# Moving the fourth batch's keys and values to a later place, and splitting the second batch's v copies between two engines, in an attention and mixture-of-experts kernel

## The chip, the cores and the metric

The kernel runs on one core of one Trainium2 chip. The metric is the device time of one execution in microseconds (us), given as the median of several runs; the range of the runs stands in brackets. Every run has a state: fast, slow, or unknown where a kernel was run only once. No run here is slow. Four kernels (e5, e6, e11, e12) have a single run of unknown state; from these only the trace is read, and their times are not compared. A ratio of two kernels is the mean time of one kernel's fast runs over that of the other's of the same rounds, so it is not quite the ratio of the medians that are quoted.

Engines carry the profile's names: PE (TensorE, matmuls), PEld (its weight loads), DVE (VectorE), ACT (ScalarE), POOL (GpSimd), SP (SyncE). All times "at" some microsecond are read from the start of the profiled span of that kernel.

## The reference, cut to what matters

```python
# q, k, v: [8 batches, 8 heads, 576 rows, 64]
def phi(x):                      # relu, times cosine and sine of the row's angle: 64 -> 128 features
    r = np.maximum(x, 0.0); return np.concatenate([r * cos, r * sin], axis=-1)
q_p, k_p = phi(q), phi(k)
kv  = einsum('bhsf,bhsd->bhfd', k_p, v);  z = k_p.sum(axis=2)
num = einsum('bhsf,bhfd->bhsd', q_p, kv)
den = einsum('bhsf,bhf->bhs', q_p, z) + 1e-6
x = (num / den) as [4608 tokens, 512]
P = exp(x @ w_gate), then 8 rounds of row and column normalisation
out = sum over 8 experts e of  P[:, e] * (relu(x @ w1[e]) @ w2[e])   # 512 -> 1024 -> 512
```

## The kernel before

The kernel has three stages: the attention of eight batches, the balancing of P, and the experts. So that TensorE never idles in the first stage, the first expert's two matrix products for batch `j` run as "block" `j`, cut into 16 slots (0 to 7 make `h`, 8 to 15 make `y`), and the attention of batch `j + 1` is put between these slots. A list says what goes where:

```python
        def at(block, slot, fn, *args):
            todo.setdefault((block, slot), []).append((fn, args))
# ... cut: after the FFN part of each slot, the tasks of that slot run in the order of registration
```

Tasks are `prep_q`, `prep_k` (relu), `prep_kp` and `prep_v` (k features, copy of v; `prep_kv` is both), `sums` (the kv and z products), `denominators`, `attend`. Moving a task in the list thus moves its work on three engines at once, and what was written later stands behind it: in e3 below, a ScalarE eviction stands behind a relu that waits 1.46 us for its load, which costs TensorE 0.39 us; in e9, VectorE's work stands 2.16 us behind a q product that waits for its buffer.

From the third batch on, q features are transposed by a DMA (a transfer by the DMA engines) on SyncE's queue, not by TensorE:

```python
            if by_dma:                                   # b >= 2
                qTs[b, hk] = q_pTs[(b * HK + hk) % len(q_pTs)]
                turned = nc.sync.dma_start(
                    out=qTs[b, hk], in_=q_p[:].rearrange("p c a d -> p (c a d)"),
                    transpose=True,
                )
```

Some of the targets are lent parts of larger tiles: in the trace the transpose of the fourth batch's third q (`hk` 2) is `acc_lo<-q_p`, and that of its fourth and last q is `acc_hi<-q_p`. The `denominators` task needs all four of them.

The next batch's inputs are loaded by GpSimd's DMA queue, six loads of 288 KB, each held back until the VectorE instruction that was written last before it has run:

```python
        def load(b, half, names="qkv", held_back=False):
            for name in names:
                # ... cut: a new tile x
                i = nc.gpsimd.dma_start(out=..., in_=...)
                if held_back:
                    after(ve.last, i)
```

And the part of the schedule for block 1 that the argument touches (batch 3 counts as the "fourth batch", batch 4 as the "fifth"):

```python
                for slot, fn, hk in (
                    (4, prep_q, 0), (5, prep_q, 1), (8, prep_k, 0), (8, prep_q, 2),
                    (9, prep_k, 1), (10, prep_kv, 0), (10, prep_k, 2), (12, prep_q, 3),
                    (12, prep_kv, 1), (12, prep_k, 3), (13, prep_kv, 2), (14, prep_kp, 3),
                    (14, prep_v, 3),
                ) if j == 1 else ( ... )
                # ... cut
                at(j, 15 if j == 1 else 14, sums, b + 1, 0)
            if j == 1:
                for name in "qkv":
                    for half in range(2):
                        at(j, 12, load, b + 2, half, name, True)   # the fifth batch's six loads
```

The last VectorE instruction of slot 12 before the loads is the v copy of `prep_kv 1` (`prep_k` runs on ScalarE). The loads hang on whatever that list has last.

Of the kernel before, what the change touches and what calls it, by code (L numbers as in the profile page):

```python
# [25 lines left out]
def kernel(  # L26
# [91 lines left out]
    te, ve, se = bound  # L118
# [62 lines left out]
    with ExitStack() as p1:  # L181
# [265 lines left out]
        def sums_begun(b, half):  # L447

            W_ = D + 1 if b else D
            if half == 0 and b:  # L450
                kvs[b] = (
                    kv_pool.tile([P, HK, 2, D], F16, name="kv_sb"),
                    kv_pool.tile([P, H, 32], F16, name="zsel"),
                )
            kv_ps = [ps_s.tile([P, 512], FP32, name="small_ps") for hh in range(2)]
            for i in range(2):
                k_p, v_aug = kps.pop((b, 2 * half + i))
                for c in range(C):
                    for hh in range(2):
                        te.matmul(  # L460
                            out=kv_ps[hh][:, i * W_ : (i + 1) * W_],
                            lhsT=k_p[hh * HP : (hh + 1) * HP, c].rearrange("p a d -> p (a d)"),
                            rhs=v_aug[hh * HP : (hh + 1) * HP, c, 0:W_],
                            start=(c == 0),
                            stop=(c == C - 1),
                        )
            return kv_ps

        def sums_made(b, half, kv_ps):
            kv_sb, zsel = kvs[b]  # L470
            W_ = D + 1 if b else D
            for hh in range(2):
                kv_v = kv_ps[hh][:, 0 : 2 * W_].rearrange("p (hk d) -> p hk d", d=W_)
                se.copy(out=kv_sb[:, 2 * half : 2 * half + 2, hh, :], in_=kv_v[:, :, 0:D])
                if b:
                    ve.tensor_tensor(
                        out=zsel[:, 4 * half + hh : 4 * half + 4 : 2, :],
                        in0=zmask[:, 4 * half + hh : 4 * half + 4 : 2, :],
                        in1=kv_v[:, :, D : D + 1].to_broadcast([P, 2, 32]),
                        op=ALU.mult,  # L480
                    )
# [106 lines left out]
        def at(block, slot, fn, *args):  # L588
            todo.setdefault((block, slot), []).append((fn, args))
# [62 lines left out]
        for j in range(B):  # L652
            b = j + 1
            if j == 0:

                def sums_first(half):
                    sums_made(1, half, sums_begun(1, half))

                for hk in range(HK):
                    for i in range(3):  # L660
                        at(0, (5, 6, 6, 7)[hk], turn, 1, hk, i, i != 1)
                    if hk == 0:
                        at(0, 5, prep_q, 1, 3)
                    if hk == 2:
                        at(0, 6, prep_v, 1, 0, se.copy)
                        at(0, 6, prep_v, 1, 2, ve.tensor_copy)
                    if hk == 3:
                        at(0, 7, prep_v, 1, 1, se.copy)
                        at(0, 7, prep_v, 1, 3, ve.tensor_copy)
                for half in range(2):  # L670
                    at(0, 7, sums_first, half)
                at(0, 8, denominators, 1)
                at(0, 10, gates, 0)
                for hk in range(HK):
                    at(0, 11 + hk, attend, 1, hk)
            elif b < B:
                if j == 1:
                    at(0, 13, load, b + 1, 0, "q", True)
                    for hk in range(HK):
                        if hk >= 2:  # L680
                            at(j, 0, prep_k, b, hk, False)
                        at(j, 0, prep_kp, b, hk)
                        at(
                            j, (0, 0, 1, 3)[hk], prep_v, b, hk,
                            (ve.tensor_copy, se.copy)[hk // 2],
                        )
                    for name, half in (("q", 1), ("k", 0), ("k", 1), ("v", 0), ("v", 1)):
                        at(j, 0, load, b + 1, half, name, True)
                    at(j, 3, sums, b, 0)
                    at(j, 5, sums, b, 1)  # L690
                else:
                    at(j, 0, sums, b, 1)
                at(j, 6 if j == 1 else 3, denominators, b)
                for hk in range(HK):
                    at(j, (9, 10, 12, 13)[hk] if j == 1 else 6 + 2 * hk, attend, b, hk)
            if j:
                at(j, 5, gates, j)
            if j == 0:
                for half in range(2):
                    at(j, 3, load, b + 1, half)  # L700
                for slot, fn, hk, *args in (
                    (8, prep_q, 0), (11, prep_k, 0), (12, prep_q, 1), (12, prep_k, 1),
                    (13, prep_q, 2), (14, prep_q, 3),
                ):
                    at(j, slot, fn, b + 1, hk, *args)
            elif b + 1 < B:
                for slot, fn, hk in (
                    (4, prep_q, 0), (5, prep_q, 1), (8, prep_k, 0), (8, prep_q, 2),
                    (9, prep_k, 1), (10, prep_kv, 0), (10, prep_k, 2), (12, prep_q, 3),
                    (12, prep_kv, 1), (12, prep_k, 3), (13, prep_kv, 2), (14, prep_kp, 3),  # L710
                    (14, prep_v, 3),
                ) if j == 1 else (
                    (4, prep_q, 0), (5, prep_k, 0), (5, prep_q, 1), (6, prep_k, 1),
                    (7, prep_q, 2), (8, prep_kv, 0), (8, prep_k, 2), (9, prep_q, 3),
                    (10, prep_k, 3), (10, prep_kv, 1), (12, prep_kv, 2), (13, prep_kv, 3),
                ) if j == 2 else (
                    (3, prep_k, 0), (4, prep_q, 0), (4, prep_k, 1), (5, prep_q, 1),
                    (7, prep_kv, 0), (7, prep_k, 2), (7, prep_q, 2), (9, prep_q, 3),
                    (9, prep_k, 3), (9, prep_kv, 1), (11, prep_kv, 2), (13, prep_kv, 3),
                ):  # L720
                    at(j, slot, fn, b + 1, hk, *((se.copy,) if fn is prep_v else ()))
                at(j, 15 if j == 1 else 14, sums, b + 1, 0)
            if j == 1:
                for name in "qkv":
                    for half in range(2):
                        at(j, 12, load, b + 2, half, name, True)
            elif j and b + 2 < B:
                for half in range(2):
                    at(j, 11 + half, load, b + 2, half, "qkv", True)
        y_pss = {}  # L730
        for j in range(B - 1):
            if j:
# [435 lines left out]
    for e in range(1, E):  # L1168
        if e == 2:
            se = nc.scalar  # L1170
        w = w_next
        for n in range(NU):
# [28 lines left out]
            if e == 1 and n == 0:  # L1201
# [9 lines left out]
                ve = nc.vector  # L1211
# [42 lines left out]
```

## Time and profile before

| what | value | where it is read |
|---|---|---|
| time | 982.96 us (982.31 to 983.07, 3 runs) | the runs |
| profiled span | 980.3 us | the page |
| PE busy | 967.1 us, 99% | the page, busy time |
| PE's share of the chain that ended last | 94% | the page, chain of waits |
| PE waits in the first 110 us that the change can touch | about 3.4 us | timeline of PE |
| first matmul of the balancing stage | 165.64 us | timeline of PE |

These lines are from the page of the kernel before: busy time of the engines, the granted TensorE clock in tenths in 40 slices of the span, and the shares of the chain of waits.

```profile
PE 967.1 (99%) x7871; PEld 674.9 (69%) x7871; DVE 806.6 (82%) x1834; ACT 564.3 (58%) x1262; POOL 60.6 (6%) x82
PEclk9999999999999999999999999999999999999999
PE 94%; DVE 2%; ACT 2%; DMA 1%; POOL 0%; issue 0%; ACTq 0%; SPq 0%; POOLq 0%
```

TensorE is the bound (967.1 of 980.3 us busy), and its granted clock is 9 tenths or more in all 40 slices (mean 0.999). The change alters none of its 7871 matmuls, only their order.

The timeline of PE shows the waits. Columns are start in us, duration in us, engine, line (L109 is the helper through which all these instructions pass), operation, tile written <- tiles read, sizes, count, and in brackets the idle time just before and what ended it. First the second batch's sums in block 0 (kernel before):

```profile
31.69 0.44 PE L109 MATMUL small_ps<-acc_lo,k_p 64*128 64x65 f16 x17 [0.34 <-DVE acc_hi L109]
32.87 1.03 PE L109 MATMUL small_ps<-acc_lo,k_p 64*128 64x65 f16 x54 [0.74 <-ACT acc_lo L109]
33.84 1.04 PE L109 MATMUL y_ps<-w2e,hT 128*128 128x512 f16 x4
```

Here PE waits 0.34 us for VectorE and 0.74 us for ScalarE's copy of v. The next lines are the same view of the kernel before, in blocks 1 and 2:

```profile
58.68 0.46 PE L109 MATMUL small_ps<-hl,acc_hi 96*128 96x192 f16 x3 [0.23 <-ACT rb L109]
...
67.50 0.46 PE L109 MATMUL small_ps<-acc_lo,k_p 64*128 64x65 f16 x18 [0.18 <-DVE acc_lo L109]
68.16 0.46 PE L109 MATMUL small_ps<-acc_lo,k_p 64*128 64x65 f16 x18 [0.21 <-DVE k_p L109]
...
72.39 0.35 PE L109 MATMUL small_ps<-acc_hi,zsel 128*32 128x192 f16 x6 [0.46 <-DMA acc_hi<-q_p]
72.66 1.90 PE L109 MATMUL h_ps<-xT,w1e 128*128 128x512 f16 x8
```

The third batch's attend waits for ScalarE (`rb`). The fourth batch's first sums wait twice for VectorE. The fourth batch's denominators wait 0.46 us for the DMA that fills `acc_hi`.

The last thing to look at is that DMA. These lines are the DMA issues of the kernel before between 64.4 and 69 us: out <- in, queue, operation, count, median us from issue to landing.

```profile
acc_lo<-q_p SPq DMA_TRANSPOSE x1, 3.3
acc_hi<-q_p SPq DMA_TRANSPOSE x1, 6.3
```

And this is the timeline of POOL, where the fifth batch's loads are issued, the first of them at 65.99 us, released by the v copy (`acc_lo`) on VectorE:

```profile
65.99 1.43 POOL L202 DMA_DIRECT2D q_ld<-in_q_dram  x2 [11.32 <-DVE acc_lo L109]
```

Both transposes move 288 KB. The one that was issued before the loads landed after 3.3 us; `acc_hi` was issued at 66.08 us, just behind the first load, and took 6.3 us.

### The profile page before, as it was taken

To read this page: it belongs to the slowest core of one execution; us is meant where nothing else is said; L and a number is where in the kernel's file an instruction comes from. 1 tells how busy PE (TensorE), PEld (TensorE's weight loads), DVE (VectorE), ACT (ScalarE), POOL (GpSimd) and SP (SyncE) were. 2 spreads that over 40 slices of the span, in tenths; PEclk is the share of its full clock that TensorE was granted. 3 is DMA by queue.
4 is the path that set the end of the run, shared out by engine and by line. 5 is a ranking of instruction groups with operands and counts; after the bars stand their busy time and mean duration, and the time that the engine had idled before them with its cause. 6 is when DMAs were issued, how large, how long until landed. Compare 5 with 4: busy or idle time off the path is not lost.

```text
span 980.3 us, 20270 instructions
## 1 busy us (share of the span) xinstructions
PE 967.1 (99%) x7871; PEld 674.9 (69%) x7871; DVE 806.6 (82%) x1834; ACT 564.3 (58%) x1262; POOL 60.6 (6%) x82
## 2 busy tenths in 40 slices
PE   9999999989999999999999999999999999999997
PEld 6545444457777777777777777777777777777775
DVE  7767774788989888988888888988888888988887
ACT  5767665467776555555555555555555555555551
POOL 6231110010000000000000000000000000000001
PEclk9999999999999999999999999999999999999999
DMA  9999881730113400223103401223103401104435
GB/s 165 184 158 172 150 134 28 145 65 33 42 33 68 93 25 25 60 59 66 49 25 69 92 25 28 63 58 66 46 25 76 85 25 34 40 26 120 127 87 129
DMA packets 80336, 73.54 MB, mean 75 GB/s; under 512 B 33264, under 2 KB 72176, under 8 KB 80240
## 3 DMA queue, kind: packets, MB, share of 16 engines
q0 software_dynamic: 27232, 30.94, 20.2%
q1 hardware_dynamic: 52768, 41.06, 16.9%
q8 instruction: 61, 1.00, 0.4%
q14 instruction: 35, 0.29, 0.1%
q10 hardware_dynamic: 240, 0.26, 0.1%
HBM read 83.12 MB, written 12.98 MB: 98 GB/s over the span
## 4 chain that ended last, share of the span: by engine, by line
PE 94%; DVE 2%; ACT 2%; DMA 1%; POOL 0%; issue 0%; ACTq 0%; SPq 0%; POOLq 0%
PE rows_ps L109 34%; PE h_ps L109 28%; PE copied_ps L109 11%; PE p_ps L109 11%; PE y_ps L109 6%; PE small_ps L109 4%; DMA acc_hi<-q_p 1%; ACT hT L109 0%; ACT acc_lo L109 0%; DVE acc_hi L927 0%; POOL hs_last L942 0%; DVE P_tok L109 0%; DMA out_dram<-acc_lo 0%; DVE colp L109 0%; ACT u L109 0%
## 5 line engine op out<-in xcount | busy, mean ns | idle before, releaser
L927 DVE SCALAR_TENSOR_TENSOR acc_lo<-rows_ps,P_tok,acc_lo 128x512 f32<-128x512 f32 (+1 forms) x322 | 203.0, 639 | 74.4 <-PE rows_ps L109 74.3
L109 PEld LDWEIGHTS <-H 128*128 128x128 f16 x2080 | 203.0, 98 | 83.1 <-issue 1.2
L863 ACT CAST u<-h_ps 128x384 f16<-128x384 f32 x288 | 137.6, 478 | 131.2 <-PE h_ps L109 131.2
L109 PEld LDWEIGHTS <-w1e 128*128 128x128 f16 x1632 | 156.4, 98 | 66.4 <-issue 6.3
L857 DVE CUSTOM_DVE_ANT_0 H<-p_ps,u 128x384 f16<-128x384 f32 x329 | 180.8, 549 | 7.0 <-PE p_ps L109 6.6
L109 PEld LDWEIGHTS <-hs 128*128 128x128 f16 x1500 | 146.5, 98 | 56.2
L109 PE MATMUL h_ps<-S,w1e 128*128 128x384 f16 x672 | 164.1, 326 | 1.1 <-ACT u L109 0.9
L109 PE MATMUL p_ps<-xT,T 128*128 128x384 f16 x672 | 164.1, 326 | 0.1
L109 PE MATMUL rows_ps<-V,H 128*128 128x256 f16 x1000 | 150.0, 273 | 0.7 <-DVE acc_hi L927 0.7
L109 PE MATMUL h_ps<-xT,w1e 128*128 128x384 f16 (+1 forms) x616 | 150.0, 350 | 0.1
L109 PE MATMUL rows_ps<-w2e,hs 128*128 128x256 f16 x1000 | 150.0, 273 | 0.0
L895 ACT ACTIVATE H<-h_ps 128x384 f16<-128x384 f32 x144 | 70.6, 490 | 95.1 <-PE h_ps L109 95.1
L109 PEld LDWEIGHTS <-T 128*128 128x128 f16 x1008 | 98.1, 98 | 29.3 <-issue 2.8
L109 PE MATMUL rows_ps<-w2e,H 128*128 128x256 f16 (+1 forms) x568 | 91.2, 285 | 0.0
L876 ACT COPY copied_ps<-h_ps 128x384 f32<-128x384 f32 x144 | 67.5, 469 | 35.3 <-PE h_ps L109 35.3
L886 ACT ACTIVATE H<-copied_ps 128x384 f16<-128x384 f32 x144 | 70.8, 492 | 20.4 <-PE copied_ps L109 20.4
L109 PE MATMUL h_ps<-S,T 128*128 128x384 f16 x336 | 81.8, 325 | 0.3 <-ACT copied_ps L109 0.3
L109 PE MATMUL copied_ps<-xT,w1e 128*128 128x384 f16 x336 | 82.1, 326 | 0.0
L109 PE MATMUL copied_ps<-w2e,H 128*128 128x256 f16 x504 | 75.5, 272 | 0.0
L109 PE MATMUL rows_ps<-V,hs 128*128 128x256 f16 x500 | 75.0, 272 | 0.0
L927 DVE SCALAR_TENSOR_TENSOR acc_lo<-copied_ps,P_tok,acc_lo 128x256 f32<-128x256 f32 x126 | 60.0, 476 | 0.5
L927 DVE SCALAR_TENSOR_TENSOR acc_hi<-rows_ps,P_tok,acc_hi 128x512 f32<-128x512 f32 (+1 forms) x56 | 41.2, 736 | 20.5 <-PE rows_ps L109 19.7
(147 smaller groups left out, 950.0 us busy)
## 6 DMA issues: line engine op xcount, KB each, us to landing
S<-x_saved SPq DMA_DIRECT2D x108, 192.0 KB, 2.4
out_dram<-acc_lo SPq DMA_DIRECT2D x62, 128.0 KB, 2.4
w1e<-in_moe_w_dram POOLq DMA_DIRECT2D x7, 1024.0 KB, 8.9
w2e<-in_moe_w_dram POOLq DMA_DIRECT2D x7, 1024.0 KB, 9.7
q_ld<-in_q_dram POOLq DMA_DIRECT2D x16, 288.0 KB, 6.4
k_ld<-in_k_dram POOLq DMA_DIRECT2D x16, 288.0 KB, 8.2
v_ld<-in_v_dram POOLq DMA_DIRECT2D x16, 288.0 KB, 9.4
x_saved<-S SPq DMA_DIRECT2D x18, 192.0 KB, 1.9
```

Source lines behind the costliest of these rows:

```text
L109: i = getattr(self.engine, name)(*args, **kwargs)
L857: latest = ve._custom_dve(TENSOR_ADD_SAT, out=out, in0=ps[:, 0:TU], in1=t[:], s0=FP32_MAX, s1=0.0)
L863: se.copy(out=t[:], in_=ps[:, 0:TU])
L876: se.copy(out=Y[:, 0:TU], in_=X[:, 0:TU])
L886: se.activation(out=h11, in_=Y[:, 0:TU], func=AF.Relu)
L895: se.activation(out=h12, in_=X[:, 0:TU], func=AF.Relu)
L927: ve.scalar_tensor_tensor(out=a, in0=rows, scalar=P_tok[:, g, self.e : self.e + 1], in1=a, op0=ALU.mult, op1=ALU.add,)
```

## The change

The intent is to remove those waits. Part A, in block 0, gives the first two v copies of the second batch to ScalarE and VectorE in turn, so that the first sums can start before the last transposes of q. Part B puts the fourth batch's k and v work later in block 1 (from slot 10 instead of 8), its sums into block 2, and its attends from slot 8 of block 2 instead of 6; the fifth batch's work in block 2 moves back by one slot.

```diff
 # part A (block 0)
                 for hk in range(HK):
+                    if hk == 3:
+                        at(0, 7, sums_first, 0)
                     for i in range(3):
                         at(0, (5, 6, 6, 7)[hk], turn, 1, hk, i, i != 1)
                     ...
-                    if hk == 2:
-                        at(0, 6, prep_v, 1, 0, se.copy)
-                        at(0, 6, prep_v, 1, 2, ve.tensor_copy)
-                    if hk == 3:
-                        at(0, 7, prep_v, 1, 1, se.copy)
-                        at(0, 7, prep_v, 1, 3, ve.tensor_copy)
-                for half in range(2):
-                    at(0, 7, sums_first, half)
+                    if hk >= 2:
+                        at(0, 4 + hk, prep_v, 1, 2 * hk - 4, se.copy)
+                        at(0, 4 + hk, prep_v, 1, 2 * hk - 3, ve.tensor_copy)
+                at(0, 7, sums_first, 1)
 # part B (blocks 1 and 2)
+                elif j == 2:
+                    at(j, 0, prep_kv, b, 3)
+                    at(j, 1, sums, b, 0)
+                    at(j, 3, sums, b, 1)
 ...
-                at(j, 6 if j == 1 else 3, denominators, b)
+                at(j, 6 if j == 1 else 5 if j == 2 else 3, denominators, b)
 ...              # attends of block 2: from slot 8 instead of 6
                 # block 1
-                    (4, prep_q, 0), (5, prep_q, 1), (8, prep_k, 0), (8, prep_q, 2),
-                    (9, prep_k, 1), (10, prep_kv, 0), (10, prep_k, 2), (12, prep_q, 3),
-                    (12, prep_kv, 1), (12, prep_k, 3), (13, prep_kv, 2), (14, prep_kp, 3),
-                    (14, prep_v, 3),
+                    (4, prep_q, 0), (5, prep_q, 1), (8, prep_q, 2), (10, prep_k, 0),
+                    (11, prep_k, 1), (11, prep_kv, 0), (12, prep_q, 3), (12, prep_k, 2),
+                    (13, prep_kv, 1), (13, prep_k, 3), (15, prep_kv, 2),
 ...              # block 2: the fifth batch's list, one slot later
-                at(j, 15 if j == 1 else 14, sums, b + 1, 0)
+                if j > 1:
+                    at(j, 15 if j == 2 else 14, sums, b + 1, 0)
 ...              # block 2's own loads one slot later too
```

The six loads of the fifth batch are still registered for slot 12 of block 1. But in the new list the last VectorE instruction of slot 12 is the q feature product of `prep_q 3`, because `prep_kv 1` has moved to slot 13.

More of the change, by code (lines that the diff above doesn't have):

```diff
@@ L690 @@
                     at(j, 5, sums, b, 1)
+                elif j == 2:
+                    at(j, 0, prep_kv, b, 3)
+                    at(j, 1, sums, b, 0)
+                    at(j, 3, sums, b, 1)
                 else:
                     at(j, 0, sums, b, 1)
-                at(j, 6 if j == 1 else 3, denominators, b)
+                at(j, 6 if j == 1 else 5 if j == 2 else 3, denominators, b)
                 for hk in range(HK):
-                    at(j, (9, 10, 12, 13)[hk] if j == 1 else 6 + 2 * hk, attend, b, hk)
+                    at(j, (9, 10, 12, 13)[hk] if j == 1 else (8 if j == 2 else 6) + 2 * hk, attend, b, hk)
             if j:
@@ L707 @@
                 for slot, fn, hk in (
-                    (4, prep_q, 0), (5, prep_q, 1), (8, prep_k, 0), (8, prep_q, 2),
-                    (9, prep_k, 1), (10, prep_kv, 0), (10, prep_k, 2), (12, prep_q, 3),
-                    (12, prep_kv, 1), (12, prep_k, 3), (13, prep_kv, 2), (14, prep_kp, 3),
-                    (14, prep_v, 3),
+                    (4, prep_q, 0), (5, prep_q, 1), (8, prep_q, 2), (10, prep_k, 0),
+                    (11, prep_k, 1), (11, prep_kv, 0), (12, prep_q, 3), (12, prep_k, 2),
+                    (13, prep_kv, 1), (13, prep_k, 3), (15, prep_kv, 2),
                 ) if j == 1 else (
-                    (4, prep_q, 0), (5, prep_k, 0), (5, prep_q, 1), (6, prep_k, 1),
-                    (7, prep_q, 2), (8, prep_kv, 0), (8, prep_k, 2), (9, prep_q, 3),
-                    (10, prep_k, 3), (10, prep_kv, 1), (12, prep_kv, 2), (13, prep_kv, 3),
+                    (5, prep_q, 0), (6, prep_k, 0), (6, prep_q, 1), (7, prep_k, 1),
+                    (8, prep_q, 2), (9, prep_kv, 0), (9, prep_k, 2), (10, prep_q, 3),
+                    (11, prep_k, 3), (11, prep_kv, 1), (13, prep_kv, 2), (14, prep_kv, 3),
                 ) if j == 2 else (
@@ L720 @@
                 ):
-                    at(j, slot, fn, b + 1, hk, *((se.copy,) if fn is prep_v else ()))
-                at(j, 15 if j == 1 else 14, sums, b + 1, 0)
+                    at(j, slot, fn, b + 1, hk)
+                if j > 1:
+                    at(j, 15 if j == 2 else 14, sums, b + 1, 0)
             if j == 1:
@@ L728 @@
                 for half in range(2):
-                    at(j, 11 + half, load, b + 2, half, "qkv", True)
+                    at(j, 11 + (j == 2) + half, load, b + 2, half, "qkv", True)
         y_pss = {}
```

## The prediction

> **What bounds it.** TensorE. The page gives PE 967.1 of 980.3 us busy and 94% of the chain of waits; the granted clock is 1.0. In the timeline of PE, four 512-column matmuls take 0.87 us, 217 ns each[...]. The change only reorders PE's instructions. So it can only remove or add PE waits in the first 110 us; everything later shifts rigidly.
>
> **Where those waits are** (timeline of PE; loss = start-to-start distance less that of the same sequence where nothing waits):
> - A, 30.55 to 33.84: second batch's sums wait 0.34 for VectorE and 0.74 for the ScalarE copy of v. Loses about 1.4.
> - B1, 57.4 to 59.7: third batch's second attend waits for ScalarE (rb), which stood until 57.09 for the landing of the fourth batch's k. Loses 0.75.
> - B2, 66.3 to 68.5: fourth batch's first sums wait for VectorE's k_p and v copies. Loses 0.64.
> - B3, 72.39: denominators wait for the transpose of the fourth batch's last q, landed 72.34. Loses 0.64.
>
> **Change B (fourth batch later), about -1.2 us.**
> - B1 goes: ScalarE's first k relu now follows the rb copies.
> - B2 goes: the sums move from slot 15 to slot 1 of the next block, where by my addition VectorE (k_p 0.67, v copy 0.37 apart) has just finished.
> - B3 stays in part. PE reaches the last heads at 72.1 by the old clock. The fifth batch's loads hang on VectorE's last instruction in slot 12; that is now q_p (64.6), not the v copy (65.7), so they are issued 1.2 us earlier. The last transpose is still issued near 66.1, behind two loads rather than one. Before, it took 6.26 us instead of about 3.3. [...]I expect landing at 72.3 to 73.5, a wait of 0.2 to 1.4.
> - VectorE then has about 11 us of work before the fifth batch's second sums; it just fits, with a possible new wait up to 0.3.
>
> Sum of B: -2.0 + 0.8.
>
> **Change A (v copies split, first sums before the last turns), about +0.6 us.** The first sums start at 31.05 (first v copy ends 31.00). The last turn needs a PSUM buffer that the first sums hold: about 0.3 wait. Worse, ScalarE now does two kv_sb copies (0.43) and two q_pT evictions (0.74) before its second v copy (0.66), which ends near 33.7 (before: 32.82). The second sums end near 34.4, against 33.84.
>
> **Prediction: 982.3 us**, 80% range 981.2 to 983.6 (before 982.96). Faster by over 2%: 0.01; within 2%: 0.98; slower by over 2%: 0.01.
>
> **What the profile would show.** Right: a PE wait of about 1.1 us near 32.6 for ScalarE's v copy, the first y_ps matmul near 34.4; no PE wait at the attends near 57 to 60 or at the sums near 66 to 69; a PE wait of 0.2 to 1.4 in the fourth batch's denominators for the transpose into acc_hi. Wrong for A: first y_ps before 33.9. Wrong for B: denominators without wait, or waiting over 2 us.
>
> **What would make it wrong.** The transpose landing after three or more loads (3 us wait, slower overall); VectorE falling behind in block 2; ScalarE's late hT evictions stalling h_ps buffers; waits in the later balancing stage moving by themselves.

Two clauses that did not come from traces of this case are cut out of it, as marked. No term of the sum goes with them: -2.0 + 0.8 us for B and +0.6 us for A, on 982.96 us, come to 982.36, put on record as 982.3. The landing at 72.3 to 73.5 us and the wait of 0.2 to 1.4 us in B3 stand as my estimate, from the 6.26 and 3.3 us named there.

## The result, and the profile after

| | before | after |
|---|---|---|
| time, median (range, runs) | 983.02 us (982.31 to 985.69, 4) | 992.57 us (991.80 to 993.43, 4) |
| profiled span | 980.3 us | 990.7 us |
| mean granted clock | 0.999 | 0.994 |
| first matmul of the balancing stage | 165.64 us | 175.93 us |
| from there to the end | 814.7 us | 814.8 us |

The ratio is 1.0092, 95% interval 1.0072 to 1.0113. That is within 2%, but the kernel became 9.6 us slower where it was predicted to become 0.7 us faster, and 992.57 lies far outside the range. The last two rows say that everything happened before the balancing stage: PE arrives there 10.29 us later, and the rest takes as long as before.

The page of the kernel after, the same three lines:

```profile
PE 969.6 (98%) x7871; PEld 675.4 (68%) x7871; DVE 807.7 (82%) x1835; ACT 564.1 (57%) x1261; POOL 60.7 (6%) x82
PEclk9997999999999999999999999999999999999999
PE 93%; DMA 2%; DVE 2%; ACT 2%; POOL 1%; issue 0%; POOLq 0%; ACTq 0%; SPq 0%
```

Read the fourth digit of PEclk: 7 where it was 9. The TensorE clock itself was lower in that slice (74 to 99 us). And DMA has gone from 1% to 2% of the chain that ended last.

Part A first, in the timeline of PE after, block 0:

```profile
31.28 0.75 PE L109 MATMUL small_ps<-acc_lo,k_p 64*128 64x65 f16 x36 [0.34 <-ACT acc_lo L109]
...
32.62 0.33 PE L109 MATMUL small_ps<-ident,q_p 128*128 128x128 f16 x3 [0.15 <-DVE zsel L109]
34.08 0.75 PE L109 MATMUL small_ps<-acc_lo,k_p 64*128 64x65 f16 x36 [1.14 <-ACT acc_lo L109]
34.76 1.04 PE L109 MATMUL y_ps<-w2e,hT 128*128 128x512 f16 x4
```

The wait of 1.14 us for ScalarE's v copy is the one that the prediction named (about 1.1). The first `y_ps` matmul starts at 34.76 us against 33.84. This execution started 0.23 us later (the first attention matmuls that need loaded data show that), so part A cost 0.69 us.

Now blocks 1 and 2 in the timeline of PE after:

```profile
59.13 0.41 PE L109 MATMUL small_ps<-hl,acc_hi 96*128 96x192 f16 x3
...
67.43 0.74 PE L109 MATMUL small_ps<-acc_lo,k_p 64*128 64x65 f16 x36
...
69.94 0.75 PE L109 MATMUL small_ps<-acc_lo,k_p 64*128 64x65 f16 x36
...
72.79 0.34 PE L109 MATMUL small_ps<-acc_lo,zsel 128*32 128x192 f16 x6
81.55 0.51 PE L109 MATMUL small_ps<-acc_hi,zsel 128*32 128x192 f16 x6 [8.43 <-DMA acc_hi<-q_p]
...
82.44 3.57 PE L109 MATMUL h_ps<-xT,w1e 128*128 128x512 f16 x8
85.81 1.91 PE L109 MATMUL y_ps<-w2e,hT 128*128 128x512 f16 x4
```

The attend at 59.13 and the sums at 67.43 and 69.94 have no bracket (the view prints none for a gap of 0.15 us or less): the waits that part B was to remove are gone. Then PE stands for 8.43 us until the transpose into `acc_hi` lands. And see what comes after: eight matmuls on `h_ps` take 3.57 us instead of 1.90, and four on `y_ps` 1.91 instead of 1.04. They run at half speed.

The windows view after shows the clock. Columns: window, length, then busy time (and count) of PE, PEld, DVE, ACT, POOL, then the granted clock, the DMA engines' busy share (which can pass 1) and GB/s.

```profile
72.00:78.00 6.00, 1.13 (x21) 0.55 (x20) 0.00 (x0) 0.89 (x2) 0.00 (x0) 0.97 1.29 157
78.00:81.00 3.00, 0.00 (x0) 0.00 (x0) 0.00 (x0) 0.00 (x0) 0.00 (x0) 0.50 1.22 199
...
83.00:85.00 2.00, 2.00 (x7) 0.65 (x5) 1.90 (x5) 0.65 (x2) 0.00 (x0) 0.50 0.00 0
...
87.00:88.00 1.00, 1.00 (x5) 0.45 (x3) 0.00 (x0) 0.22 (x1) 0.00 (x0) 0.59 1.11 210
88.00:89.00 1.00, 1.00 (x8) 0.45 (x8) 0.45 (x1) 0.70 (x2) 0.00 (x0) 1.00 1.07 204
```

PE has nothing to do from 73.1 us on; by 78 us the granted clock is 0.50, and it stays there until about 87.8 us, over 6 us after PE was busy again (81.55 us). The clock records of the packed trace put the fall at 77.59 us, 4.5 us after PE had run out of work, and the return at 87.83 us.

How long the half clock lasts differs between executions. In after it lasted 10.24 us, and full clock came back 6.3 us after PE had resumed. In e10 below, after a wait of 7.43 us, the granted clock was 0.95 from 90 to 94 us, 0.50 from 94 to 98 and 0.69 from 98 to 102; from these shares I estimate 6.9 us of half clock, which ended near 100.5 us, 3.1 us after PE had resumed. In e5, after a wait of 3.33 us, eight matmuls on `h_ps` took 3.43 us, and the four on `y_ps` behind them, from 80.90 us on, 1.03 us again: full clock was back no later than 4.0 us after PE had resumed. In e4 and e6, after waits of 8.13 and 6.61 us, the eight matmuls on `h_ps` took 3.38 and 3.33 us, 1.5 and 1.4 us more than the 1.90 of before. In after those eight alone lost 1.7 us, and the `y_ps` ones behind them were slow too. So the 2.8 us of the table below belong to this execution.

These are the DMA issues after, between 64.4 and 69 us:

```profile
acc_lo<-q_p SPq DMA_TRANSPOSE x1, 6.1
acc_hi<-q_p SPq DMA_TRANSPOSE x1, 14.5
```

And where the fifth batch's loads are issued (timeline of POOL after):

```profile
65.86 1.43 POOL L202 DMA_DIRECT2D q_ld<-in_q_dram  x2 [10.26 <-DVE q_p L109]
```

They are now released by `q_p`, not by the v copy. In the kernel's own sequence that is earlier: `acc_hi` was issued at 66.08 before and at 66.99 after, 0.91 us later; the first load at 65.99 and 65.86, 0.13 us earlier. So the loads have moved about 1.0 us ahead of the transposes. Two loads are now issued before `acc_hi` (65.86 and 66.57; the third at 67.28). As predicted. What was not predicted is what that does: 14.5 us instead of 6.3.

What the time was made of, on PE's timeline up to the balancing stage. Each "loss" is a start-to-start distance less that of the same pair of instructions where nothing waits:

| item | us |
|---|---|
| later start of this execution | +0.23 |
| part A | +0.69 |
| the three waits of before in blocks 1 and 2, gone | -2.03 |
| the wait for `acc_hi` | +8.6 |
| matmuls at half clock after that wait | +2.8 |
| sum | +10.3 |
| first matmul of the balancing stage, 175.93 - 165.64 | +10.29 |

### How the transpose is slowed

The records of the DMA queues give packet sizes. A transpose is 1152 packets of 256 bytes; a load is 256 packets of 1152 bytes (as the profiler counts packets). Both move 288 KB. The next two lines are the DMA queues of the kernel after from 76 to 80 us, with packets, MB, and busy share of the 16 engines. q0 carries the loads, q1 the transpose:

```profile
q0 software_dynamic: 581, 0.63, 90.9%
q1 hardware_dynamic: 583, 0.15, 27.6%
```

In those 4 us the two queues went one for one: 581 packets to 583. But a packet of the loads has 4.5 times as many bytes as a packet of the transpose, so the loads moved 0.63 MB and the transpose 0.15 MB. At that ratio the 1152 packets of a transpose go beside about 1152 load packets, which is 4.5 whole loads (an estimate from these counts). Counted over the whole transfer, 1197 load packets began between the first and the last data packet of `acc_hi`. It landed at 81.51 us, the moment at which the fifth load (the first of v) landed.

Why did it take only 6.3 us before? These are the same queue lines of the kernel before from 70 to 72 us:

```profile
q1 hardware_dynamic: 994, 0.25, 67.2%
q0 software_dynamic: 192, 0.20, 59.1%
```

From 68 to 70 us the two queues went one for one there too (183 packets to 181). Then the first q load was through (last packet at 70.66 us) and the second began to send only at 71.28 us: around that gap 994 transpose packets ran in 2 us, and `acc_hi` landed at 72.34 us. In this execution the transpose slipped through a gap between two loads. After, issued behind one more load, it got no gap. The gap is not the whole reason, as the next paragraphs show.

One thing more is needed for the whole length. The transposes share one queue, and in after even the third q's one, `acc_lo`, took 6.1 us instead of 3.3, although by 69.0 us 2304 data packets had been begun since the second q's transpose went out, which is all of that one and all of `acc_lo`. On that queue the 47 packets from 69 to 71.6 us are 31 of 4 bytes and only 16 of data; the first data packet of `acc_hi` came at 70.97 us, though it was issued at 66.99. The loads' queue sent 233 packets from 69 to 71 us. What held the first packet back was not shown: no run tests it.

The packets of all the traces give a sharper dividing line than the gap. In the six executions in which `acc_hi` took 9 us or more (after, and e2, e4, e5, e6 and e7 below), the first load packet began 0.3 to 0.5 us before the last data packet of `acc_lo`; `acc_lo` then took 5.4 to 6.2 us, and all of `acc_hi` came behind it. In the other seven (before, e1, e3, e8, e9, e11, e12) it began after that packet, and `acc_lo` took 3.3 to 3.4 us. In after the two packets are at 68.34 and 68.74 us, in before at 67.48 and 67.40. In before, e1 and e11 the margin was under 0.1 us, so before stands close to the edge. This is a line drawn through thirteen traces; no run places the loads within that margin on purpose.

### The profile page after: what moved, and what is told of

Read it like the earlier page. It is cut to its first block, busy times and chain, and to the rows that moved or that the text cites. A ratio compares the mean times of both kernels' runs of the same rounds, so it can differ in the third digit from the quotient of the medians.

```text
span 990.7 us, 20271 instructions
## 1 busy us (share of the span) xinstructions
PE 969.6 (98%) x7871; PEld 675.4 (68%) x7871; DVE 807.7 (82%) x1835; ACT 564.1 (57%) x1261; POOL 60.7 (6%) x82
## 4 chain that ended last, share of the span: by engine, by line
PE 93%; DMA 2%; DVE 2%; ACT 2%; POOL 1%; issue 0%; POOLq 0%; ACTq 0%; SPq 0%
PE rows_ps L109 34%; PE h_ps L109 27%; PE copied_ps L109 11%; PE p_ps L109 11%; PE y_ps L109 6%; PE small_ps L109 4%; DMA acc_hi<-q_p 1%; DMA k_ld<-in_k_dram 1%; ACT hT L109 0%; DVE acc_hi L929 0%; POOL hs_last L944 0%; DVE P_tok L109 0%; DMA out_dram<-acc_lo 0%; DVE colp L109 0%; ACT u L109 0%
## 5 line engine op out<-in xcount | busy, mean ns | idle before, releaser
L109 PE MATMUL copied_ps<-w2e,H 128*128 128x256 f16 x504 | 75.5, 272 | 0.0
```

The costliest lines, as they stand in the source:

```text
L109: i = getattr(self.engine, name)(*args, **kwargs)
```

## The experiments

Theory 1 (T1): part B puts the fifth batch's loads ahead of the last transpose; the transposing queue then goes packet for packet with the loads (583 beside 581 in 4 us of after); the wait and the half clock that follows it make the whole loss. Rivals: part A, or both parts together, cost it (T2); the reordering of TensorE, VectorE and ScalarE in part B costs it, the DMA being only where it shows (T3); the delay is fixed, or ends with the first loads, and does not depend on how many loads there are (T4). The expectations call these by their own names, but it is the same set. "y0" or "first y_ps" below is the start of the second expert product in block 0, the marker for part A.

### The parts alone: e1_a_only and e2_b_only

The edit of e1 is the first hunk of the diff above, and nothing else; that of e2 is all the rest.

> Only the first part of the change: second batch's v copies split, its first sums ahead of the last turns. The result's trace put the first y_ps matmul 0.92 us later than before, of which 0.22 was there by 14.3 us, ahead of the change. Theory (load collision in part B): this part alone costs 0.7 us, all of it between 31 and 35 us, and no large wait anywhere; 983.7 us against 983.0. Rival (the two parts need each other, or part A shifts transfers into a collision): over 986 us.

> Only the second part: fourth batch later, v copies as before. Theory: the fifth batch's loads still hang on VectorE's q_p of slot 12, so they still come 0.4 us after the issue of the transpose into acc_lo and ahead of the one into acc_hi; the latter lands about 14.5 us after its issue, the fourth batch's denominators wait 8.4 us, then a half-speed TensorE clock costs about 2.8; 992.0 us in all, 0.7 less than the changed kernel. Rival (the wait came of both parts together): within 1 us of the kernel before.

| | median (range, runs) | ratio to before | wait for `acc_hi` | its time from issue |
|---|---|---|---|---|
| before, same job | 983.41 (982.63 to 984.53, 7) | | | |
| part A alone | 983.56 (983.55 to 985.84, 4) | 1.0008 (0.9993 to 1.0023) | 0.85 us | 6.6 us |
| part B alone | 991.27 (990.10 to 992.01, 4) | 1.0080 (1.0064 to 1.0097) | 8.50 us | 14.4 us |

Part A alone shows its 0.34 and 1.14 us waits and a first `y_ps` at 34.72 us, 0.68 us late after the offset of its start. In run times these 0.7 us cannot be told from nothing (ratio 1.0008, interval on both sides of 1); the timeline alone shows them. Part B alone brings the collapse; its timeline of PE has this line:

```profile
81.49 0.51 PE L109 MATMUL small_ps<-acc_hi,zsel 128*32 128x192 f16 x6 [8.50 <-DMA acc_hi<-q_p]
```

Rival T2 falls.

### One slot for the loads: e3_after_loads13

```diff
 # against the kernel after
-                        at(j, 12, load, b + 2, half, name, True)
+                        at(j, 13, load, b + 2, half, name, True)
```

> The changed kernel with one number changed: the fifth batch's loads are issued at slot 13 of block 1 in place of slot 12; no compute instruction moves. They then hang on VectorE's second k_p/v copy and come at about 67.4 us, after both transposes (65.5 and 67.0) are issued. Theory: the transpose into acc_hi lands 3.3 to 5 us after its issue (before 72.5), the denominators don't wait, the clock stays at 1.0, and about 11 us come back: 981.7 us. Rival 1 (the new order of VectorE and TensorE work in block 2 itself costs time): stays over 985. Rival 2 (a transpose in flight beside any six loads takes 14 us, whichever is issued first): stays at 992.

Measured: 983.01 us (982.38 to 984.12, 4 runs), ratio to before 0.9998 (0.9983 to 1.0013). The lines of this kernel: PE at the denominators, POOL at the loads, and the DMA issue of `acc_hi`.

```profile
73.16 0.34 PE L109 MATMUL small_ps<-acc_hi,zsel 128*32 128x192 f16 x6
```

```profile
67.79 1.43 POOL L202 DMA_DIRECT2D q_ld<-in_q_dram  x2 [12.05 <-DVE acc_lo L109]
```

```profile
acc_hi<-q_p SPq DMA_TRANSPOSE x1, 4.6
```

The loads are issued at 67.79, after `acc_hi` (67.19). It lands in 4.6 us, the denominators have no bracket any more, and the mean clock is back at 0.999. One number in the source takes 9.6 us away (by the medians, 992.57 to 983.01). This shows that the loads' place, not the reordering of the engines, makes the loss.

It also missed its expectation by 1.3 us: 981.7 had been expected. The trace shows what was forgotten: 1.2 us of new waits in block 2. One is 0.39 us for ScalarE, whose `hT` eviction stands behind a k relu that waits for its load (landed at 76.9); the others are 0.17, 0.30 and 0.30 us at the attends for VectorE, which has too much to do there. In the kernel after they don't show, since PE stands anyway while the others catch up.

### The loads alone, in the kernel before: e4_before_loads_early

The reverse: the kernel before, with the six loads registered right behind `prep_q 3` of slot 12. No other instruction changes its place on any engine.

```diff
 # against the kernel before
                     at(j, slot, fn, b + 1, hk, *((se.copy,) if fn is prep_v else ()))
+                    if (j, slot, fn, hk) == (1, 12, prep_q, 3):
+                        for name in "qkv":
+                            for half in range(2):
+                                at(j, 12, load, b + 2, half, name, True)
 # ... and the six loads of block 1 at their old place taken out
```

> The kernel before with nothing changed but what the fifth batch's loads hang on: VectorE's q_p of slot 12 (ends 64.6) in place of the v copy of slot 12 (ends 65.7), so they are issued at about 65.0 in place of 66.0. Theory: the 1 us is enough; the transpose into acc_hi lands near 80.6 in place of 72.3, the denominators wait some 8.8 us in place of 0.5, the clock halves; 994 us, worse than the changed kernel, as the old waits of block 1 stay. Rivals (order of compute, later slots): 983 us.

Measured: 992.87 us (991.84 to 993.28, 4 runs), ratio 1.0095 (1.0080 to 1.0110). Its denominators on PE, and its DMA issue:

```profile
80.51 0.51 PE L109 MATMUL small_ps<-acc_hi,zsel 128*32 128x192 f16 x6 [8.13 <-DMA acc_hi<-q_p]
```

```profile
acc_hi<-q_p SPq DMA_TRANSPOSE x1, 14.0
```

The loads went out at 65.41 us instead of 65.99; `acc_hi` at 66.50, and landed at 80.47. Nothing else was changed, and the loss is as large as that of the full change. Together with e3 this shows that in these two kernels the early loads are enough to make the loss, and that it goes when they are taken away; T3 falls.

### Fewer loads beside the transpose: e5_after_2loads and e6_after_4loads

```diff
 # against the kernel after (e5; e6 has "qk" first and only "v" late)
-                for name in "qkv":
+                for name in "q":
                     for half in range(2):
                         at(j, 12, load, b + 2, half, name, True)
+                for name in "kv":
+                    for half in range(2):
+                        at(2, 6, load, b + 2, half, name, True)
```

> The changed kernel, but only the two q loads of the fifth batch are issued at slot 12; its four k and v loads hang on slot 6 of block 2, after the denominators. Only the landing of the transpose into acc_hi counts here; what follows will be late. Theory: from about 71.6 us the DMA engines take one 256-byte packet of the transpose for one 1152-byte packet of a load, as long as there are loads. The transpose has 1152 packets, a load 256, so with six loads it ends with the load that is four and a half further (81.5). With only q's second load left it should share 256 packets and then run alone at some 1000 packets a us: landing at 74 to 76, wait of PE 1 to 3 us. Rival (a fixed delay, once a load is issued between the two transposes): 81.5 as before.

> The same with q and k at slot 12 and only v's two loads late. Theory (one packet for one packet): three loads are left at 71.6 us, 768 of the 1152 packets go beside them, the rest alone: landing at 77 to 78.5, wait of PE 4 to 5.5 us. Rival (fixed delay): 81.5. Rival (the transpose lands as soon as the loads issued before it, q's two, are in): 76.2 or earlier, the same as with two loads.

The one packet for one in both is measured in after: 1170 packets on the transposes' queue beside 1189 on the loads', from 71.5 to 80.9 us. The 1000 packets a us fit before, where the transposes' queue, with no load beside it, sent 2000 packets from 80 to 82 us.

The DMA issue of `acc_hi`, first with two loads beside it, then with four:

```profile
acc_hi<-q_p SPq DMA_TRANSPOSE x1, 9.2
```

```profile
acc_hi<-q_p SPq DMA_TRANSPOSE x1, 12.5
```

With two loads it was issued at 67.68 and landed at 76.88 us, with four 67.48 and 79.94, with six (the kernel after) 66.99 and 81.51. The waits of PE are 3.33, 6.61 and 8.43 us. The delay grows with the number of loads: had it been fixed, all would have landed at about 81.5; had it ended with q's loads, e5 and e6 would be alike. T4 falls in both forms. In e5, from 74 to 76 us, when the two loads were through, the transpose's queue sent 776 packets in 2 us, against 583 in 4 us beside loads.

The packet counts fit the theory closely: beside the 1152 data packets of `acc_hi` 246 load packets began with two loads, 738 with four and 1197 with six (expected 256, 768 and 1152).

Both landed later than expected (74 to 76, and 77 to 78.5), by 0.9 and 1.4 us. Part of that is the way from the last data packet to the landing, 1.0 us in e5 and 0.5 us in e6, which the expectation left out. In e6, as in the other traces of the collision with more than two loads, both queues also slow down sharply or stop for about half a microsecond between 75.5 and 76.5 us; the record gives no reason. Their times (995.97 and 991.34 us; before in that job 986.19, 983.84 to 988.47, 7 runs) are not to be compared with the rest: e5 pays 6.26 us later on for its late k loads, as had been said beforehand.

### The clock by itself: e7_after_warm

The wait is filled with 37 matmuls of 512 columns that go nowhere, so that PE doesn't idle.

```diff
 # against the kernel after; stay_warm(n) is n matmuls of ones into an unused y_ps buffer
+                if j == 2:
+                    at(j, 5, denominators, b, range(0, 6))
+                    at(j, 5, stay_warm, 37)
+                    at(j, 5, denominators, b, range(6, 8))
```

> The changed kernel with 37 matmuls of 512 columns on constants, whose result nobody reads, put into the wait ahead of the last two heads' denominators (8.0 us at 217 ns). Theory: the long wait itself stays (transpose lands near 81.5), but TensorE does not fall to half clock, so the 2.8 us of half-speed matmuls after it go: 989.8 us, granted clock 1.0 throughout. Rival (the slow matmuls after the wait have another cause, such as DMA traffic): 992.5.

Measured: 991.85 us (991.57 to 992.14, 4 runs), ratio 1.0061 (1.0040 to 1.0082). In the timeline of PE of this kernel:

```profile
81.75 0.34 PE L109 MATMUL small_ps<-acc_hi,zsel 128*32 128x192 f16 x6 [0.75 <-DMA acc_hi<-q_p]
...
82.44 1.89 PE L109 MATMUL h_ps<-xT,w1e 128*128 128x512 f16 x8
84.17 1.03 PE L109 MATMUL y_ps<-w2e,hT 128*128 128x512 f16 x4
```

The granted clock stays at 1.00, and the same matmuls take 1.89 and 1.03 us instead of 3.57 and 1.91. From the denominators to the balancing stage PE needs 92.36 us instead of 94.38. Of the 2.8 us that the half clock cost, 2.7 came back, and 0.67 was lost again to a new wait for VectorE at 93.46 us, which the slow matmuls had hidden. So the second item of the sum is shown too, in size, on the timeline. The run times cannot show it: the kernel after was not run in this job, and before's runs of the job were high (median 986.19 us). The total missed its expectation (989.8): another 1.06 us was lost after the balancing stage had begun, which no other of these kernels shows but for small parts of it. The filler takes a turn of the `y_ps` buffers and so shifts which buffer each later product gets; whether that is the cause was not tested and stays open.

### Versions with later loads: e8, e9, e10

e8 is part B alone with the loads at slot 13 (the edits of e2 and e3 together).

> The second part of the change without the first, with the fifth batch's loads at slot 13. Theory by sum: part A's 0.7 us are saved against the third experiment (983.0 there, 0.1 less than before on the PE's timeline up to the balancing stage), so 982.3; the three waits of the kernel before are gone (2.0 us), and about 1.2 of new ones stay in block 2 (VectorE behind the attends, ScalarE waiting for k).

Measured: 982.30 us (980.86 to 982.50, 4 runs). Its ratio to before, 0.9961 (0.9934 to 0.9987), flatters it: before's runs of that job were high (median 986.19 us). On PE's timeline the balancing stage starts at 165.73 us against before's 165.64. What part B takes away in blocks 1 and 2 (2.0 us) it gives back in new waits of block 2: 0.96 us for ScalarE behind a k relu that waits for its load, the rest for VectorE.

e9 mends what these traces show: the two VectorE v copies and the ScalarE ones of block 0 placed so that neither half waits; in block 2 the k relus after the attend of slot 8; two v copies on ScalarE.

```diff
 # against the kernel after
 # block 0: as before, but v copies 0 and 3 on ScalarE, 1 and 2 on VectorE:
+                        at(0, 6, prep_v, 1, 0, se.copy)
+                        at(0, 6, prep_v, 1, 1, ve.tensor_copy)
+                        at(0, 6, prep_v, 1, 2, ve.tensor_copy)
 ...                      # hk == 3:
+                        at(0, 7, prep_v, 1, 3, se.copy)
 # block 2, fifth batch:
-                    (5, prep_q, 0), (6, prep_k, 0), (6, prep_q, 1), (7, prep_k, 1),
-                    (8, prep_q, 2), (9, prep_kv, 0), (9, prep_k, 2), (10, prep_q, 3),
-                    (11, prep_k, 3), (11, prep_kv, 1), (13, prep_kv, 2), (14, prep_kv, 3),
+                    (5, prep_q, 0), (6, prep_q, 1), (8, prep_k, 0), (8, prep_q, 2),
+                    (9, prep_k, 1), (10, prep_k, 2), (10, prep_q, 3), (11, prep_kv, 0),
+                    (12, prep_k, 3), (12, prep_kp, 1), (12, prep_v, 1), (13, prep_kp, 2),
+                    (13, prep_v, 2), (15, prep_kv, 3),
 # and the loads of block 1 at slot 13; prep_v of these lists on ScalarE
```

> The second part with the fifth batch's loads at slot 13, and what the earlier runs showed as left-over waits moved: in block 0 the second batch's first v copy on ScalarE, the next two on VectorE, the last on ScalarE, turns ahead of the sums as before (first y_ps 33.2 to 33.5 against 33.84); in block 2 ScalarE's k relus after the attend of slot 8, so that they no longer hold up hT while k is in flight, and two v copies of the fifth batch on ScalarE. Expected on PE's timeline up to the balancing stage: 0.4 to 0.6 from block 0 and 1.6 to 2.0 from blocks 1 and 2; no wait over 0.3 us between 55 and 170 us; 980.7 us where the kernel before takes 983.0, a ratio of 0.998. Rival (the loads now collide elsewhere, or ScalarE falls behind): over 982.5 or a new wait of over 0.5 us.

Measured: 981.35 us (980.98 to 982.04, 6 runs; 980.7 had been expected) against before's 983.96 (982.38 to 988.46, 11 runs) in that job: ratio 0.9971 (0.9950 to 0.9992). Three of before's eleven runs lie at 987 to 988.5 us; without them the means are 981.46 and 983.27, ratio 0.998. All six runs lie below the fastest of before in that job. It is the fastest version that was found, though by no more than two or three tenths of a per cent against before, and before's own profiled execution, in another job, took 982.04 us. The first `y_ps` starts at 33.41 us (expected 33.2 to 33.5), so the block 0 part did what the original part A set out to do. Blocks 1 and 2 gave nothing, where 1.6 to 2.0 us had been expected: the balancing stage starts at 165.25 us, 0.39 earlier than before (0.54 after the later start of this execution), and block 0 alone accounts for that. A new wait of 1.36 us remains at 84.59 us, for VectorE, which had itself stood 2.16 us in a q product for a free `q_p` buffer (held by a transpose from 76.15 to 82.19).

e10 moves that one q product in block 2 from slot 10 to slot 13, to take this wait away.

```diff
 # against e9, block 2
-                    (9, prep_k, 1), (10, prep_k, 2), (10, prep_q, 3), (11, prep_kv, 0),
-                    (12, prep_k, 3), (12, prep_kp, 1), (12, prep_v, 1), (13, prep_kp, 2),
-                    (13, prep_v, 2), (15, prep_kv, 3),
+                    (9, prep_k, 1), (10, prep_k, 2), (11, prep_kv, 0), (12, prep_k, 3),
+                    (12, prep_kp, 1), (12, prep_v, 1), (13, prep_kp, 2), (13, prep_v, 2),
+                    (13, prep_q, 3), (15, prep_kv, 3),
```

> The ninth experiment's kernel with one step moved: the q_p of the fifth batch's last head pair goes from slot 10 to slot 13 of block 2. In the ninth it stood on VectorE for 2.2 us, until the transpose of the first head pair (third and last q_p buffer in turn) had landed at 82.2, and TensorE waited 1.36 us for the attend's product behind it. Expected: that wait is below 0.3, PE's first matmul of the balancing stage comes 1.2 us sooner than in the ninth (164.0 against 165.25), 980.2 us. Rival (the wait only moves to the fifth batch's sums or to its denominators): 981.3 as the ninth.

Measured: 989.64 us (989.29 to 990.87, 5 runs), ratio 1.0064 (1.0050 to 1.0077): a clear miss, and an instructive one. Its timeline of PE in block 3, and the DMA issue of the transpose that it waits for:

```profile
97.39 0.51 PE L109 MATMUL small_ps<-q_pT,zsel 128*32 128x192 f16 x6 [7.43 <-DMA q_pT<-q_p]
97.83 2.74 PE L109 MATMUL h_ps<-xT,w1e 128*128 128x512 f16 x6
```

```profile
q_pT<-q_p SPq DMA_TRANSPOSE x1, 12.9
```

This is the same collision one batch later. The fifth batch's last transpose now goes out at 84.45 us, behind the sixth batch's loads (82.77, 83.48, 84.19 and on), and lands at 97.35 us. PE waits 7.43 us, and then runs at half clock: six matmuls in 2.74 us. In e9 that transpose went out at 83.11 us and the first of these loads at 85.77; the one moved product brought the loads forward by 3.0 us and put the transpose back by 1.3. I made the same mistake again, in another block, when I moved a transpose behind loads while looking only at the engines' waits. It agrees with T1 at a place that the change doesn't touch; no further run took the loads away there.

### The kernel before twice more: e11_before_again and e12_before_again

Some of before's runs took 987 to 988.5 us in two of the jobs. If the transpose sometimes missed its gap, a profile might catch it.

> The kernel before, unchanged, once more. Some of its executions on the later chips took 987 to 988.5 us, at a granted clock of 0.996 to 0.998, where most took 982.4 to 984.3; the kernels with the loads at slot 13 showed no such run. Theory: it stands close to the same collision; in its slow executions the transpose into acc_hi lands after 76 us and the denominators wait 4 us or more. A fast execution here decides nothing. Rival: a slow execution without such a wait.

> The same once more, for the same reason: a slow execution should show the transpose into acc_hi landing after 76 us; a fast one near 72.3 to 74.

Both were single runs of ordinary length (983.29 and 983.36 us); `acc_hi` went from 66.84 to 73.53 and from 66.38 to 73.59 us, and PE waited 0.89 and 1.25 us. No long run was caught. In e12 the loads left no gap, and `acc_hi` still took no more than 7.2 us: 542 of its 1152 packets had gone out by 68.5 us, before many load packets were sent. They decide nothing about the long runs, and why before sometimes takes 5 us longer stays open. The margin of under 0.1 us found above would fit, but no long run was profiled.

## Why the prediction was wrong, point by point

- TensorE as the bound, and "everything later shifts rigidly": right. From the balancing stage to the end 814.7 us before, 814.8 after. But "it can only remove or add PE waits" forgot that a long wait also changes the rate: the granted clock fell to 0.50 and cost another 2.8 us in the profiled execution (e7 gave 2.7 of it back).
- Part A, "+0.6 us" with a 1.1 us wait for ScalarE's v copy: right. 0.69 us in after, 0.68 alone, and the wait is 1.14.
- "B1 goes", "B2 goes": right. No bracket at these attends and sums after.
- "B3 stays in part ... I expect landing at 72.3 to 73.5, a wait of 0.2 to 1.4": this is the step that failed. Its premise was right: the loads hang on `q_p`, and the transpose is issued behind two loads rather than one. The size was wrong: landing 81.51 us, wait 8.43. I counted the packets of neither queue. Before, the transpose had taken about 3 us longer behind one load, and a second load ahead of it was costed as 0 to 1.2 us more. But before was no measure of what a load costs: its transpose had escaped through a gap, with most of the loads still to come. A transpose has 1152 packets, six loads have 1536, so once it goes packet for packet with them (583 to 581 in 4 us of after) it lasts for about 4.5 loads (1197 load packets were counted). And it began late: `acc_lo` ahead of it on the same queue, which the prediction did not look at, took 6.1 us instead of 3.3.
- "The transpose landing after three or more loads (3 us wait)" stood under what would make it wrong: the right place, at a third of the size, and with no weight in the range.
- VectorE "just fits, with a possible new wait up to 0.3": mis-sized. With the collision taken out (e3), block 2 has 1.2 us of new waits, 0.77 of them for VectorE and 0.39 for ScalarE. So without the collision the change would have been worth about nothing: 983.01 us.
- The stated test "Wrong for B: denominators without wait, or waiting over 2 us" is met by its second half.

What stays open: the half microsecond in which both queues slow down or stop, the 1.06 us that e7 lost after the balancing stage began, why `acc_hi`'s first data packet came 3.98 us after its issue, and before's long runs.

## What to carry to other kernels

When tasks are moved in a list, look at what else hangs on "the last instruction before here": here six loads moved ahead of a transpose because a copy left their slot. Where two DMA queues are busy at once, count packets, not bytes: here 583 packets of one went beside 581 of the other in 4 us, so the transpose with its packets of 256 bytes moved 0.15 MB while the loads with theirs of 1152 moved 0.63, and its mild 6.3 us in the first profile came out of a gap. And a wait of TensorE of several microseconds can cost more than itself: in these traces waits of 3.3 to 8.4 us were followed by half clock (eight 512-column matmuls in 3.33 to 3.57 us instead of 1.90), and full clock was back 3.1 us (e10, estimated above) to 6.3 us (after) after PE had resumed.
